# Three weight slots converted anew in the second pair, and output blocks that take PSUM banks 4 to 7 first

## The chip, the cores and the metric

The kernel runs on one core of a Trainium2 chip. The metric is the device time of one execution in microseconds (us). A smaller time is better.

## What is computed

Attention over local chunks (4 batches, 8 heads, 768 positions, head size 64, 8 memory positions), then two feed-forward layers over the 3072 rows that result:

```python
scores = scale * np.matmul(q_c, k_full.transpose(0, 1, 3, 2))   # chunks of 32, 16 left, 8 right, 8 memory
out[:, :, c_start:c_end] = np.matmul(softmax(scores), v_full)
...
h = x @ w_in                                  # [3072,512] @ [512,2048]
x = (h * np.tanh(softplus(h))) @ w_out        # [2048,512]
...
xn = x / rms * rms_g
g = xn @ w_gate                               # [512,1536]
return (silu(g) * (xn @ w_val)) @ w_out2      # [1536,512]
```

The weights arrive as 64-bit floats and are turned into 32-bit ones on the chip. Each matrix product is done with three matmuls, on a rounded high part and a low part of each operand (hi by hi, hi by lo, lo by hi).

## The kernel before

**Tiling.** The 3072 rows are 8 blocks of 384 and 4 pairs of blocks. A pair is multiplied with a pair of weight columns by a scheme of seven products in place of eight (`group`, from L572): products 1, 6, 5, 4, 2, 7, 3 in that order, on four PSUM banks X, Y, Z, V. VectorE, ScalarE and GpSimd take the results out. Seven products need seven weight blocks, each with a high and a low part: a weight slot of 1792 KB.

**The w_in slots.** The eight slots ("i", 0) to ("i", 7) share five places in SBUF (`W_SLOT`): 0 and 5 in place 0, 1 and 6 in place 4, 2 and 7 in place 3, slot 3 in place 2, slot 4 in place 1. A slot is first converted "plain" (`cv_all`): two 512 KB loads of raw 64-bit columns (tile raw, two buffers), and for each two ScalarE passes (L180, L183), three VectorE passes (L187, L188, L194) and a split into high and low parts (L140 ScalarE, L141 VectorE). That gives the four blocks themselves. `finish` (from L249) makes the other blocks out of them: it adds the halves back together (L254), forms four sums on GpSimd (L259, L260) and VectorE (L261, L262) and splits them. A job of the kind "pair" does all in one: two raw loads, conversion, sums and splits of seven blocks. Its block order is `W_AT`; that of a finished plain slot is `W_IN`.

**Stages.** A prologue starts the attention and the first products. *Stage 1* (about 60 to 156 us in the profile) multiplies pair 0 with plain slots, eight products by block (`unit`), with the attention of pair 1 between the products. *Stage 2* (156 to 246) is pair 1 over the slots 7 to 0 with the attention of pair 2 in between, *stage 3* (246 to 320) is pair 2 over 0 to 7 with the attention of pair 3, *stage 4* (320 to 390) is pair 3 over 7 to 1, with the conversion of w_out in between. Then come the w_out products of the 8 blocks (`out1`), which accumulate in four banks each (`banks1`), the gate and value products (`group2`) and the last product (`group3`).

**Order.** The function `between` that `slots` returns runs after each product (a step). It sends stores that are due, runs what `more` holds for that step, gives out attention pieces, and drives the conversion to a given count (`cv_upto`). The tile framework then orders each engine's instructions by a simulated time line, apart from those under `pin` or `in_start`; so a step is a place in the program and not a time.

**Places of slots.** In stage 1, `finish` of slots 0, 1, 2 stands right after their use, and `keep_w` stores each slot to DRAM (tensor wi) in two stores of 896 KB (L124). Slot 7 is finished at the end of stage 1, slots 6, 5, 4, 3 at steps 1, 8, 15, 22 of stage 2, where slots 7, 6, 5 are stored. `reload` (L119) loads the slots 2, 1, 0 in stage 2 after the first three groups, 5, 6, 7 in stage 3, and 2, 1, 0 again in stage 4.

**Queues.** All DMAs are issued by SyncE's queue (SP) in one order: raw loads (L136), loads of queries (L314), keys (L304), values (tile vw, eight loads of 56 KB a tile, L335), stores of products (g_scratch, L105), and stores and loads of slots.

**Banks.** Attention uses banks 4 to 7. The groups of pairs 1 to 3 use banks 0 to 3 (`group_banks(4)`); block m of w_out uses banks 0 to 3 if m is even and 4 to 7 if it is odd.

Of the kernel before, what the change touches and what calls it, by code (L numbers as in the profile page):

```python
# [24 lines left out]
W_AT = {1: 0, 2: 1, 4: 2, 3: 3, 5: 4, 6: 5, 7: 6}  # L25
W_IN = {1: 0, 2: 1, 3: 2, 4: 3, 5: 4, 6: 5, 7: 6}
# [3 lines left out]
def tile_kernel(  # L30
# [24 lines left out]
    N = 384  # L55
# [96 lines left out]
    def add_plain(key, arr, f0, f1, u):  # L152
        jobs.append(("plain", key, [(arr, "col", f0), (arr, "col", f1)], u, True, False))
# [348 lines left out]
    def att_list(j):  # L502

        out = []
        t0 = TPP * j
        for s in range(TPP + 4):
            for op, lag in (("e", 4), ("d", 3), ("c", 2), ("b", 1), ("a", 0)):
                t = t0 + s - lag
                if t0 <= t < t0 + TPP:
                    if op == "a" and t % SPB == 0:  # L510
                        out.append([(att_a0, t)])
                    out.append([(att_ops[op], t), (att_ops[op + "1"], t)])
        return out
# [45 lines left out]
    def product(at, w, t, bank_, first):  # L559
        ws = w[:, at].rearrange("p l (k f) -> p l k f", k=2)  # L560
        ps = bank_[:, 0:N]
        for kk in range(2):
            whi, wlo = ws[:, 0, kk, :], ws[:, 1, kk, :]
            xh, xl = t[:, 0, kk, :], t[:, 1, kk, :]
            more = dict(skip_group_check=not first)
            nc.tensor.matmul(ps, whi, xh, start=first and kk == 0, stop=False, **more)  # L566
            nc.tensor.matmul(ps, whi, xl, start=False, stop=False, **more)  # L567
            nc.tensor.matmul(ps, wlo, xh, start=False, stop=kk == 1, **more)  # L568
# [41 lines left out]
    def unit(b, i):  # L610
        need(("i", i))
        w = wtab["i", i]
        g = gp.tile([128, 2, N], F32, tag="g", name="g")
        for e in range(2):
            ps = bk[(2 * n_unit[0] + e) % 4]
            for half in range(2):
                product(2 * e + half, w, xtab[b, half], ps, half == 0)
                if half:
                    nc.scalar.copy(g[:, e, :], ps[:, 0:N])
                    if e:  # L620
                        store_later(
                            g_d[0, 2 * i:2 * i + 2, :, b, :].rearrange("f p n -> p f n"), g
                        )
                yield
        n_unit[0] += 1

    def run(parts, between):
        while parts:
            for part in list(parts):
                if next(part, "end") == "end":  # L630
                    parts.remove(part)
                else:
                    between()
# [3 lines left out]
    def group_banks(of):  # L637
        g = n_group[0]
        n_group[0] += 1
        return [bk[(4 * g + i) % of] for i in range(4)]  # L640

    def group1(j, i, between):
        run([group1_parts(j, i)], between)
# [1 line left out]
    def group1_parts(j, i):  # L645
        need(("i", i))
        g = [gp.tile([128, 2, N], F32, tag="g", name="g") for _ in range(2)]
        ts = {p: ttab_x[j, p] for p in ORDER}
        mul = lambda p, bank_, first: product(W_IN[p], wtab["i", i], ts[p], bank_, first)
        banks = group_banks(4)  # L650
        c11 = banks[0][:, 0:N]
        yield from group(mul, banks, N, g[0][:, 1, :], g[1][:, 0, :], g[1][:, 1, :])
        nc.scalar.copy(g[0][:, 0, :], c11)
        for e in range(2):
            store_later(g_d[j, 2 * i + e], g[e])
# [50 lines left out]
            return self.out.pop(0)  # L706

    def banks1(m):
        return [bk[(4 * m + c) % 8][:, 0:N] for c in range(KC)]

    def out1(m, i, t):
        for e in range(2):
# [96 lines left out]
    down = up[::-1]  # L809
    for i in (0, 1, 2, 3, 4, 5, 7, 6):  # L810
        add_plain(("i", i), w_in, 2 * i, 2 * i + 1, W_SLOT[i])
    for f, u in zip(range(0, F1, 3), (5, 6, 7, 1, 2, 3)):
        fs = range(f, min(f + 3, F1))
        add_rows([("o1", x) for x in fs], w_out, fs, u)
# [42 lines left out]
    def slots(pieces, conv, tail=(), more={}, cap=10 ** 6):  # L857


        state = dict(n=0, att=0, tail=0)  # L860
        plist, n_slots = pieces
        first_cv, to = conv
        base = cv_n[0]

        def between():
            state["n"] += 1
            n = state["n"]
            flush()
            if n in more:
                more[n]()  # L870
            span = n_slots - 7
            while state["att"] < len(plist) and state["att"] * span < n * len(plist):
                for fn, t in plist[state["att"]]:
                    fn(t)
                state["att"] += 1
            if n > first_cv:
                cv_upto(min(cap, base + (to - base) * (n - first_cv) // (n_slots - first_cv)))
            if n >= n_slots - 7 and tail:
                if state["tail"] == 0:
                    state["t"] = tail()  # L880
                    for fn in state["t"][0]:
                        fn()
                elif state["tail"] <= len(state["t"][1]):
                    state["t"][1][state["tail"] - 1]()
                state["tail"] += 1

        return between

    def tail_of(j):
        return lambda: t_pieces(j, xb.pop(2 * j), xb.pop(2 * j + 1), t_new, None, ttab_x)  # L890

    def keep_w(i, half):
        return lambda: w_store(("i", i), half)

    def reload(pos, seq):
        if pos < 3:
            w_load(("i", seq[5 + pos]), W_SLOT[seq[5 + pos]])
# [3 lines left out]
    def then(more, n, fn):  # L901
        more.setdefault(n, []).append(fn)

    def finish_at(more, i, n):
        part = finish(("i", i))
        for step in range(3):
            then(more, n + step, lambda: next(part))

    def calls(more):
        return {n: (lambda fns=fns: [fn() for fn in fns]) for n, fns in more.items()}  # L910
# [2 lines left out]
    units += [(b, i) for i in (2, 3, 4, 5, 7, 6) if i >= NHEAD for b in range(2)]  # L913
    at = {u: 4 * n + 4 for n, u in enumerate(units)}
    more = {}
    for i in range(3):
        finish_at(more, i, at[1, i] + 1)
        for half in range(2):
            then(more, at[1, i] + 4 + 3 * half, keep_w(i, half))
    finish_at(more, 7, at[1, 7] + 1)  # L920
    bt = slots((att_list(1), 4 * len(units)), (0, 73), tail_of(1), calls(more), CV_I)
    for b, i in units:
        run([unit(b, i)], bt)
    more = {}
    for i, ns in ((7, (3, 5)), (6, (9, 12)), (5, (16, 19))):
        for half, n in enumerate(ns):
            then(more, n, keep_w(i, half))
    for n, i in enumerate((6, 5, 4, 3)):
        finish_at(more, i, 7 * n + 1)
    bt = slots((att_list(2), 56), (0, 0), tail_of(2), calls(more))  # L930
    for pos, i in enumerate(down):
        group1(1, i, bt)
        reload(pos, down)
    bt = slots((att_list(3), 56), (0, 0), tail_of(3))
    for pos, i in enumerate(up):
        group1(2, i, bt)
        reload(pos, up)
    att_stack.close()
    w2p[0] = ctx.enter_context(
        tc.tile_pool(name="w2p", bufs=1, side="right", reuse_waits="tile")  # L940
# [173 lines left out]
```

## Time and profile before

| | us |
|---|---|
| median of three runs | 1208.36 (1205.7 to 1210.33) |
| the profiled execution | 1208.05 |
| its span in the profile | 1206.3 |
| TensorE busy in the span | 1164.7 (97%) |
| VectorE busy | 820.8 (68%) |
| ScalarE busy | 623.3 (52%) |
| GpSimd busy | 210.5 (17%) |

Busy times are of an engine's own instructions. What an idle stretch of TensorE (PE) waited for stands in brackets in a row of the time line: the time, and the instruction that ended the wait. PEclk is the granted clock of TensorE as a share of 2.4 GHz, which has two levels, 1.2 and 2.4 GHz; DMA is the mean busy share of the core's 16 DMA engines.

### The profile page before, as it was taken

How to read it: one execution, taken by the hardware profiler on the slowest of the kernel's cores; microseconds unless marked ns; L12 is line 12 of the kernel's file. 1: busy time of each engine (PE TensorE's matmuls, PEld its weight loads, DVE VectorE, ACT ScalarE, POOL GpSimd, SP SyncE). 2: the span in 40 equal slices, each digit the busy share in tenths (PEclk: the TensorE clock that was granted, in tenths of full speed). 3: DMA queues.
4: the chain of work that ended last, by engine and by line, in shares of the span. 5: the costliest groups of instructions: out<-in, count | busy, mean ns of one | idle time of the engine just before them, and what ended most of it. 6: DMA issues, size and time to landing. Idle time of an engine off the chain costs nothing.

```text
span 1206.3 us, 24873 instructions
## 1 busy us (share of the span) xinstructions
PE 1164.7 (97%) x9944; PEld 1128.4 (94%) x9944; DVE 820.8 (68%) x1331; ACT 623.3 (52%) x1055; POOL 210.5 (17%) x203
## 2 busy tenths in 40 slices
PE   5899889999999999999999999999999999999998
PEld 4788779888998999999999989999999999999998
DVE  3676695563676866668586876676667665987773
ACT  4565454343456874776866554443434433444442
POOL 2030131111134311111101222212122211100000
PEclk8799989999999999999999999999999999999999
DMA  9999889778387843858559788888397669755540
GB/s 184 207 260 268 223 253 295 206 215 248 104 345 268 294 146 121 324 176 300 192 179 410 289 335 341 321 331 332 109 356 276 267 223 337 190 161 141 141 132 36
DMA packets 216052, 287.50 MB, mean 238 GB/s; under 512 B 103552, under 2 KB 181376, under 8 KB 211712
## 3 DMA queue, kind: packets, MB, share of 16 engines
q1 hardware_dynamic: 215936, 285.91, 71.7%
q8 instruction: 78, 1.28, 0.4%
q14 instruction: 38, 0.31, 0.1%
HBM read 180.49 MB, written 105.38 MB: 237 GB/s over the span
## 4 chain that ended last, share of the span: by engine, by line
PE 81%; DMA 7%; DVE 6%; ACT 3%; issue 2%; SPq 1%; POOL 0%; DVEq 0%; ACTq 0%; POOLq 0%
PE bk L566 13%; PE bk L567 12%; PE bk L568 12%; PE bk L674 4%; PE bk L673 4%; PE bk L675 4%; PE bk L786 4%; PE bk L787 4%; PE bk L788 4%; DMA raw<-in_moe_w_in_dram 2%; PE bkp L566 2%; PE bkp L568 2%; PE bkp L567 2%; PE bkp L675 2%; PE bkp L674 2%; PE bkp L673 2%
## 5 line engine op out<-in xcount | busy, mean ns | idle before, releaser
L566 PE MATMUL bk<-T,w 128*128 128x384 f32 x992 | 340.3, 345 | 4.8 <-DMA T<-nt_scratch 1.8
L567 PE MATMUL bk<-T,w 128*128 128x384 f32 x992 | 335.1, 338 | 0.0
L568 PE MATMUL bk<-T,w 128*128 128x384 f32 x992 | 331.3, 337 | 0.1
L566 PEld LDWEIGHTS bk<-T,w 128*128 128x128 f32 x992 | 187.3, 189 | 10.6 <-DMA T<-nt_scratch 2.8
L567 PEld LDWEIGHTS bk<-T,w 128*128 128x128 f32 x992 | 187.7, 189 | 0.9
L568 PEld LDWEIGHTS bk<-T,w 128*128 128x128 f32 x992 | 186.9, 189 | 0.5 <-DVE w L141 0.4
L673 PE MATMUL bk<-T,w 128*128 128x384 f32 x384 | 130.6, 342 | 1.7 <-DVE s L593 1.7
L674 PE MATMUL bk<-T,w 128*128 128x384 f32 x384 | 129.9, 338 | 1.7 <-DVE T L141 1.7
L675 PE MATMUL bk<-T,w 128*128 128x384 f32 x384 | 129.4, 337 | 0.0
L786 PE MATMUL bk<-w,T 128*128 128x256 f32 x396 | 111.7, 282 | 0.0
L788 PE MATMUL bk<-w,T 128*128 128x256 f32 x396 | 111.4, 282 | 0.0
L787 PE MATMUL bk<-w,T 128*128 128x256 f32 x396 | 111.3, 281 | 0.0
L593 DVE TENSOR_TENSOR s<-bk,s 128x384 f32<-128x384 f32 (+1 forms) x84 | 45.0, 536 | 91.2 <-PE bk L568 81.7
L597 POOL TENSOR_TENSOR v<-s,z 128x384 f32<-128x384 f32 x48 | 53.2, 1109 | 193.5 <-DVE s L593 128.4
L141 DVE TENSOR_TENSOR T<-g,T 128x768 fp32r<-128x768 f32 x64 | 66.0, 1048 | 20.9 <-ACT T L140 20.8
L674 PEld LDWEIGHTS bk<-T,w 128*128 128x128 f32 x384 | 72.7, 189 | 3.1 <-DVE T L141 2.3
L787 PEld LDWEIGHTS bk<-w,T 128*128 128x128 f32 x396 | 75.5, 191 | 0.0
L673 PEld LDWEIGHTS bk<-T,w 128*128 128x128 f32 x384 | 72.6, 189 | 2.9 <-ACT ca L180 2.0
L786 PEld LDWEIGHTS bk<-w,T 128*128 128x128 f32 x396 | 75.2, 190 | 0.0
L141 DVE TENSOR_TENSOR T<-w,T 128x768 fp32r<-128x768 f32 x60 | 58.8, 991 | 23.9 <-ACT T L140 23.1
L788 PEld LDWEIGHTS bk<-w,T 128*128 128x128 f32 x396 | 75.1, 190 | 0.0
L140 ACT CAST T<-w 128x768 fp32r<-128x768 f32 x60 | 49.3, 833 | 47.5 <-PE bk L788 28.4
(158 smaller groups left out, 2358.1 us busy)
## 6 DMA issues: line engine op xcount, KB each, us to landing
T<-nt_scratch SPq DMA_DIRECT2D x49, 768.0 KB
g_scratch<-g SPq DMA_DIRECT2D x64, 384.0 KB
g<-g_scratch SPq DMA_DIRECT2D x64, 384.0 KB
h_scratch<-s SPq DMA_DIRECT2D x48, 384.0 KB
w<-h_scratch SPq DMA_DIRECT2D x24, 768.0 KB
w<-wi SPq DMA_DIRECT2D x9, 1792.0 KB
nt_scratch<-T SPq DMA_DIRECT2D x21, 768.0 KB
raw<-in_moe_w_out_dram SPq DMA_DIRECT2D x28, 512.0 KB
```

The lines of the kernel that those rows point to most:

```text
L140: keep(nc.scalar.copy(hi, src))
L141: keep((eng or nc.vector).tensor_tensor(lo, src, hi.bitcast(F32), op=ALU.subtract))
L566: nc.tensor.matmul(ps, whi, xh, start=first and kk == 0, stop=False, **more)
L567: nc.tensor.matmul(ps, whi, xl, start=False, stop=False, **more)
L568: nc.tensor.matmul(ps, wlo, xh, start=False, stop=kk == 1, **more)
L597: nc.gpsimd.tensor_tensor(c22, u3, z5, op=ALU.add)
L673: nc.tensor.matmul(ps, ahi, bhi, start=start, stop=False)
L674: nc.tensor.matmul(ps, ahi, blo, start=False, stop=False)
L675: nc.tensor.matmul(ps, alo, bhi, start=False, stop=stop)
L786: nc.tensor.matmul(ps, t[:, 0, f], w[:, 0], start=first and f == 0, stop=False, **more)
L787: nc.tensor.matmul(ps, t[:, 0, f], w[:, 1], start=False, stop=False, **more)
L788: nc.tensor.matmul(ps, t[:, 1, f], w[:, 0], start=False, stop=f == HG - 1, **more)
```

## The change

Slots 0, 1 and 2 are no longer finished and stored in stage 1. They are dropped after their plain use and converted again from the raw columns by three "pair" jobs, which stand in the conversion's order between the plain jobs and w_out. Those 33 steps of conversion are spread over steps 12 to 45 of stage 2; the reloads of stage 2 go. The finishes of slots 6, 5, 4, 3 move to steps 1, 4, 7, 10. Slots 0, 1, 2 are stored in stage 3, at steps 1 to 17, for the reloads of stage 4. From stage 2 on these three slots are read in the order `W_AT`. The three entries that do nothing (`lambda: None`) add nothing.

Blocks of w_out with an even m take banks 4 to 7, those with an odd m banks 0 to 3, and the groups with eight banks begin with 4 to 7 in place of 0 to 3. `group_banks(4)` gives the same banks as before.

```diff
-        return [bk[(4 * g + i) % of] for i in range(4)]
+        return [bk[(4 * g + of - 4 + i) % of] for i in range(4)]
...
-        mul = lambda p, bank_, first: product(W_IN[p], wtab["i", i], ts[p], bank_, first)
+        at = W_AT if i < 3 else W_IN
+        mul = lambda p, bank_, first: product(at[p], wtab["i", i], ts[p], bank_, first)
...
     def banks1(m):
-        return [bk[(4 * m + c) % 8][:, 0:N] for c in range(KC)]
+        return [bk[(4 * m + 4 + c) % 8][:, 0:N] for c in range(KC)]
...
+    for i in (2, 1, 0):
+        add_pair(("i", i), w_in, 2 * i, w_in, 2 * i + 1, W_SLOT[i], True, False)
...
-    for i in range(3):
-        finish_at(more, i, at[1, i] + 1)
-        for half in range(2):
-            then(more, at[1, i] + 4 + 3 * half, keep_w(i, half))
     finish_at(more, 7, at[1, 7] + 1)
...
+    for i in range(3):
+        del wtab["i", i]
...
     for n, i in enumerate((6, 5, 4, 3)):
-        finish_at(more, i, 7 * n + 1)
-    bt = slots((att_list(2), 56), (0, 0), tail_of(2), calls(more))
-    for pos, i in enumerate(down):
+        finish_at(more, i, 3 * n + 1)
+    for n, i in ((8, 2), (15, 1), (22, 0)):
+        then(more, n, lambda: None)
+    bt = slots((att_list(2), 56), (12, CV_I + 33 + 11), tail_of(2), calls(more), CV_I + 33)
+    for i in down:
         group1(1, i, bt)
-        reload(pos, down)
-    bt = slots((att_list(3), 56), (0, 0), tail_of(3))
+    more = {}
+    for i, ns in ((0, (1, 3)), (1, (8, 10)), (2, (15, 17))):
+        for half, n in enumerate(ns):
+            then(more, n, keep_w(i, half))
+    bt = slots((att_list(3), 56), (0, 0), tail_of(3), calls(more))
...
+    CV_I += 33
```

## Rows read from the trace of the kernel before

**Rows 1.** The page: the span.
```profile
span 1206.3 us, 24873 instructions
```
**Rows 2.** Stages: window, its length, busy us (instructions) of each engine, clock, DMA.
```profile
60.00:110.00 50.00, 49.14 (x713) 45.74 (x713) 37.40 (x76) 33.88 (x64) 9.15 (x10) 1.00 0.91 268
110.00:156.00 46.00, 36.77 (x534) 33.01 (x540) 29.77 (x52) 20.94 (x40) 8.41 (x8) 0.95 0.88 225
156.00:246.00 90.00, 88.04 (x1231) 80.14 (x1212) 59.54 (x112) 41.58 (x77) 15.73 (x18) 0.97 0.84 255
246.00:320.00 74.00, 72.57 (x1103) 66.03 (x1104) 35.77 (x74) 27.45 (x50) 7.57 (x7) 1.00 0.68 199
390.00:1206.00 816.00, 806.40 (x5080) 801.15 (x5080) 573.69 (x871) 428.04 (x705) 138.56 (x127) 1.00 0.67 239
```
**Rows 3.** Time line of TensorE, 110 to 157 us: start, length, instruction, [wait before].
```profile
119.64 0.66 PE L490 MATMUL bk<-ident,x 128*128 128x128 f32 x4 [1.67 <-ACT qT L405]
...
137.52 0.79 PE L490 MATMUL bk<-ident,x 128*128 128x128 f32 x4 [1.57 <-DVE x L480]
...
155.70 0.89 PE L415 MATMUL bkp<-kw,qT 64*32 64x64 f32 x38 [3.81 <-DVE kw L360]
```
**Rows 4.** Waits of ScalarE, 60 to 156 us: total, times, longest.
```profile
ACT ca L180 <- DMA raw<-in_moe_w_in_dram: 15.5, 6, 5.7
```
**Rows 5.** The chain that ended last, 100 to 140 us: start, length, what.
```profile
111.47 6.41 DMA raw<-in_moe_w_in_dram
...
134.31 3.95 DMA raw<-in_moe_w_in_dram
```
**Rows 6.** Time line of SP's queue, stages 1 and 2: start, time to issue, what.
```profile
102.06 0.69 SPq L124 DMA_DIRECT2D wi<-w  x1
102.84 7.43 SPq L335 DMA_DIRECT2D vw<-in_v_dram  x8
110.33 1.04 SPq L124 DMA_DIRECT2D wi<-w  x1
...
128.31 5.89 SPq L335 DMA_DIRECT2D vw<-in_v_dram  x8
...
149.42 1.70 SPq L335 DMA_DIRECT2D vw<-in_v_dram  x4
...
208.99 10.60 SPq L335 DMA_DIRECT2D vw<-in_v_dram  x8
```
**Rows 7.** DMA view of 80 to 112 us.
```profile
DMA packets 10299, 9.30 MB, mean 291 GB/s; under 512 B 7321, under 2 KB 9639, under 8 KB 10294
```
**Rows 8.** VectorE's groups, 60 to 110 us: count, busy us, mean ns, idle before.
```profile
L188 DVE SCALAR_TENSOR_TENSOR ca<-raw,ca 128x512 int32<-128x512 int32 x6 | 4.1, 686 | 0.1
L194 DVE CUSTOM_DVE_ANT_0 ca<-ca,lr 128x1024 uint16<-128x1024 uint16 x6 | 4.1, 684 | 0.2
L141 DVE TENSOR_TENSOR w<-sm,w 128x768 fp32r<-128x768 f32 (+1 forms) x6 | 3.9, 680 | 0.0
...
L187 DVE TENSOR_SCALAR ca<-ca 128x512 int32<-128x512 int32 x6 | 2.5, 409 | 2.8 <-ACT ca L180 2.8
```
**Rows 9.** Stretches of 10 us around both changes of stage, columns as in rows 2.
```profile
150.00:160.00 10.00, 5.95 (x83) 4.60 (x82) 9.20 (x12) 6.49 (x12) 4.30 (x3) 0.75 0.94 276
160.00:170.00 10.00, 10.00 (x112) 9.23 (x112) 10.00 (x21) 5.30 (x11) 1.44 (x2) 0.91 0.48 144
...
390.00:400.00 10.00, 9.48 (x46) 9.51 (x47) 8.57 (x12) 8.20 (x14) 5.41 (x4) 0.83 0.90 309
```
**Rows 10.** Time line of VectorE at the change to stage 2.
```profile
151.28 1.92 DVE L141 TENSOR_TENSOR w<-sm,w 128x768 fp32r<-128x768 f32 x2
```
**Rows 11.** Time line of TensorE late in stage 2.
```profile
229.55 1.38 PE L464 MATMUL bkp<-vw,pT 64*32 64x65 f32 x12 [1.24 <-DMA vw<-in_v_dram]
```
**Rows 12.** Time lines of TensorE and VectorE at the first w_out block.
```profile
390.52 0.66 PE L673 MATMUL bk<-T,w 128*128 128x384 f32 x1 [1.70 <-DVE s L593]
...
388.95 0.96 DVE L141 TENSOR_TENSOR T<-g,T 128x768 fp32r<-128x768 f32 x1 [2.16 <-ACT T L140]
```

## The prediction

> **What bounds the kernel now.** I read the stages first [rows 1, 2]. TensorE is busy for 1164.7 us of 1206.3 by the table, and its work isn't changed by more than bank numbers. So all that the change can win is idle time and time at the lower clock, in the places that it touches. From 390 us on, 806.40 of 816 us are busy; before 60 us nothing is touched. Between lie these losses: 0.9 us in 60 to 110, 9.2 us in 110 to 156, 2.0 in stage 2, 1.4 in stage 3 (each is the window's length less PE busy).
>
> Then I looked at what ended those waits. In 110 to 156 there are four waits before 140 us (1.67 us the first, 1.57 the last), each for a different ScalarE or VectorE result, and one of 3.81 us at 155.70 [rows 3]. The four come to 5.0 us. Behind all four is one thing: ScalarE stands at L180 and waits for raw columns, 15.5 us in six times, 5.7 the longest [rows 4]. An engine that works in order holds back everything queued behind such a wait, here the evictions and the attention's copies that TensorE needs. The chain of waits says the same: it runs through the raw loads, 6.41 us from issue to landing at 111.47, 3.95 us at 134.31 [rows 5]. And SP's queue tells why they are issued late: right ahead of the one at 111.47 stand two slot stores (0.69 and 1.04 us) and, between them, eight value loads that took 7.43 us [rows 6].
>
> The wait at 155.70 is of another kind. It is VectorE's queue at the change of stage: key copies for the attention stand behind the sums of the next pair and behind a finish, of which two splits alone take 1.92 us [rows 10]. After it the clock is at the lower level: 0.75 and 0.91 in the two stretches [rows 9] make 2 x (0.25 + 0.09) x 10 = 6.8 us at 1.2 GHz, about 6 of them with TensorE at work, so 3.0 us more are lost.
>
> **The change part by part.** Sums are made against the profiled execution's 1208.05 us, 0.3 us under the median of 1208.36.
>
> *Stage 1, stores and finishes removed.* Six stores of 896 KB go, 5.4 MB. All DMA of 80 to 112 us is 9.30 MB at 291 GB/s [rows 7], so they are some 18 of those 32 us (5.4 / 9.3 of them). On SP's queue the raw load at 111.47 comes at least 0.69 + 1.04 = 1.7 us earlier. The value loads between are not of fixed length either: 0.93 us each there, 0.43 each at 149.42 with fewer transfers about, 1.33 each at 208.99 [rows 6]. At 0.43 the eight take 3.4 us in place of 7.4, 4.0 us more. So the raw load comes 1.7 to 5.7 us earlier, and each later one hangs on the one before. The four waits (5.0 us) shrink by 1.7 to 5.0; I take 4.0, nearer to the upper end since most of the bytes about are gone. With them goes time at the lower clock: 0.95 over 46 us [rows 2] is 4.6 us at that level, most of it right after the fourth wait and partly idle; I take 0.7 us, of 0 to 0.9. The finishes taken out free VectorE of 3.9 us of splits [rows 8] and the sums before them in 60 to 110, where TensorE lost only 0.9 us: nothing gained. Together **-4.7**, from -1.7 to -5.9.
>
> *Change to stage 2.* Slot 7's finish stays where it is. If the conversions end earlier, its passes come before the last attention tile and not in the middle of the sums; if the finishes of 5 and 4, now at steps 4 and 7, are drawn forward, one more pair of splits (1.92 us) stands ahead of the key copies. Bounds: +1.9 to -6.8 (the 3.8 us of idle time and the 3.0 us of clock). Nothing shows which, so I take a small part, **-1.3**. The four finishes packed into 12 steps fall where VectorE is busy 10.00 of 10 us already with TensorE busy 10.00 too [rows 9]: a full VectorE alone didn't stall it. **+0.3**, from 0 to 1.9.
>
> *Stage 2, three conversions added.* Each raw half costs VectorE 0.41 + 0.69 + 0.68 = 1.78 us [rows 8]; two halves, two small sums and four splits at about 0.68 or a little less make about 7 us a slot, 21 us in all. VectorE's 59.54 of 90 us [rows 2] become 80, or 89%. ScalarE, at 41.58 of 90, has more room still, and GpSimd's two sums a slot only move from stage 1 to here. By the 10.00 of rows 9 the added work itself is hidden. What can stall is what stalls in stage 1: a raw load that comes late. The first two are issued in stage 1, where w_out's stood. Each later one is issued when its buffer is read, and is wanted ten steps later, at some 90/56 = 1.6 us a step 16 us later; in stage 1 it was eight steps, 13 us. Value loads of 7 us ahead of it and a landing of 6.4 us make 13 to 14. So it was short there and just suffices here. **+1.0**, from 0 to 5.0, what the same cause costs in stage 1.
>
> *Stage 2, reloads removed.* Three loads, 5.4 MB, become six raw loads, 3.1 MB. The value loads that take 10.60 us at 208.99 should fall back to about 7, and the wait for values at 229.55, 1.24 us [rows 11], with them. SP no longer stands at L119 until a group has released its place. **-1.2**, from 0 to -1.2.
>
> *Stage 3, stores added.* The 5.4 MB come at steps 1 to 17, beside loads of 5.4 MB; DMA is at 0.68 there and TensorE loses 1.4 us now [rows 2]. It becomes what stage 2 is today: **+0.5**, from 0 to 1.2 (the one value wait of rows 11). The reloads of stage 4 find the data there long before.
>
> *Banks.* At the first w_out block TensorE waits 1.70 us until 390.52, for the reading of a bank of the last group [rows 12]. With banks 4 to 7, unused since stage 3, it needs only the operand T, whose low half is ready at 388.95 + 0.96 = 389.91. So 0.6 us are won if it must wait for that, 1.7 if the order lets it start with the high half, and the clock's 0.83 behind it [rows 9], 3.4 us at the lower level and 1.7 lost, may stay away too. I take **-0.7**, from -0.6 to -3.4. Later blocks alternate as before: nothing.
>
> Sum: -4.7 - 1.3 + 0.3 + 1.0 - 1.2 + 0.5 - 0.7 = -6.1, 1208.05 - 6.1 = **1202.0**.
>
> **The rivals.**
> 1. *SP's issue time is the limit, whatever the bytes.* Then the value loads of stage 1 stay at 7 us, the raw loads come 1.7 us earlier and no more, nothing is won at the change of stage or at 229.55: -1.7 + 0.3 + 1.0 + 0.5 - 0.7 = -0.6, **1207.5**. For it: eight such loads still take 5.89 us at 128.31, after the last store [rows 6]. Against it: 0.43, 0.93 and 1.33 us for one and the same load. The Trainium skill, "Perfetto Trace Analysis", section "What DMA-bound means", has this as its second case: an issuer's track that is solid DMA slices is bound by the making of descriptors and not by data movement. By that rule the time is the one above; the spread of rows 6 speaks against it here. Chance 0.22.
> 2. *The wait moves to stage 2* (slower). Six raw loads come in where slot stores of 7, 6, 5, product stores and value loads already go. If a raw load lands later than 16 us after its buffer is free, ScalarE stands at L180 with evictions of all four banks behind it, as in stage 1, where four raw loads cost 5.0 us, 1.25 each. Six cost 7.5 us, and the clock falls as it did at 155 us, 3.0 more: 10.5 in place of 1.0. With the value wait kept too (+1.2), -6.1 + 9.5 + 1.2 = +4.6, **1212.7**. For it: value loads of 10.60 us in this stage today. Against it: fewer bytes and longer steps. Chance 0.13.
> 3. *The change of stage closes up.* If slot 7's finish is over before the last attention tile, the sums start at once, and both the idle time and the clock loss go nearly whole: -6.0 in place of -1.3, **1197.3**. Against it: other finishes are drawn forward into the gap. Chance 0.15.
> 4. *It doesn't do what it says.* The framework orders engines by its own time line; the moved steps may land where they were, and gains and losses cancel: **1208**. Chance 0.05.
>
> **How the numbers follow.** The forecast has 0.45, its own range 1199 to 1205 (terms half a step to either bound). Below 1196.5 I leave 0.08 (rival 3 with the clock at the first w_out block), above 1211 0.12 (most of rival 2). A measurement can tell 0.5% from no change, 6.0 us: faster means below 1202.3. Of the forecast a little over half lies there, with rival 3 that makes 0.42; slower (above 1214.4) is the upper half of rival 2 and what I overlook, 0.09; the rest, 0.49, is within.
>
> **What would show it.** Right: no or short waits of L180 before 140 us, no wait over 1 us in 110 to 140; the first w_out matmul waits for T and not for a group's result; no wait for values near 229 us; VectorE near 90% in stage 2 with TensorE's idle time under 2 us. Wrong: L180 waiting for w_in in 160 to 230 us (rival 2), value loads of 0.9 us each still in stage 1 (rival 1). The forecast hangs most on stage 1 and on the change of stage, where VectorE's order is made by the framework and can't be read from here.

## The result, and the profile after

The changed kernel takes 1191.17 us (median of six, 1188.33 to 1195.78) beside 1210.36 for the kernel before in the same session (1205.7 to 1215.05): a ratio of 0.9872, 95% interval 0.9843 to 0.9901. That is faster by 1.3%, and it lies below the range of the prediction, 1196.5 to 1211. The sign was right, and the size was low by 11 us. The profiled execution took 1190.82 us, 17.2 less than that of before.

Where the time came from is read best from points of the program that both kernels pass: the starts of the groups of a pair, of the w_out blocks and of the later products. My count of the matmul records in the two profiles, in us:

| stretch | before | after | change | forecast |
|---|---|---|---|---|
| before the first w_in product | 44.50 | 45.22 | +0.7 | 0 |
| from there to the first group of pair 1 (stage 1 and the wait at its end) | 112.01 | 102.30 | -9.7 | -6.0 |
| stage 2 | 89.35 | 83.70 | -5.65 | +0.1 |
| stage 3 | 83.15 | 83.83 | +0.7 | +0.5 |
| stage 4, to the first w_out matmul | 61.51 | 59.96 | -1.55 | -0.7 with the next |
| first w_out block | 34.95 | 33.91 | -1.0 | |
| the other w_out blocks | 240.67 | 241.50 | +0.8 | 0 |
| gate and value products and the last product | 535.74 | 533.87 | -1.9 | 0 |

The forecast of -6.0 is the prediction's -4.7 and -1.3; part of the latter is clock at the start of stage 2. The last two kinds of product stand in one row because they overlap: 24 matmuls of the gate and value products run after the first matmul of the last product in before, and 6 in after. At the end of stage 1, 38 score matmuls of the attention (the last row of [rows 3], 0.89 us) run ahead of the border in before and behind it in after. By this count stage 3 of before ends at 329.0 us, and not at 320.

How far such lengths repeat is read from the kernels below whose edits leave a stage alone: there every engine has the same instructions in the same order. Stage 1 of after takes 102.30 to 104.44 us in six profiles (after, e2, e8, e12, e13, e15) and 107.13 in a seventh (e7); that of before takes 111.38 to 115.93 in three (before, e1, e6). Stage 2 of after takes 83.48 to 84.59 in four (after, e2, e9, e12), that of before 87.28 to 89.35 in the same three. So both stages are shorter beyond chance. The differences of the means are 9.3 and 4.6 us, and a difference of a us or two between two profiles means nothing.

The stages of the kernel after, by windows (columns as in [rows 2]):

```profile
60.00:110.00 50.00, 49.14 (x715) 45.68 (x714) 29.76 (x61) 32.72 (x61) 4.40 (x4) 1.00 0.88 232
110.00:148.00 38.00, 34.84 (x515) 32.52 (x514) 29.40 (x50) 19.84 (x36) 8.29 (x8) 1.00 0.82 195
148.00:232.00 84.00, 83.78 (x1197) 77.23 (x1196) 76.80 (x146) 51.84 (x98) 20.53 (x23) 0.98 0.83 249
232.00:316.00 84.00, 83.36 (x1196) 76.22 (x1195) 45.84 (x89) 35.11 (x63) 9.41 (x9) 1.00 0.78 246
376.00:1189.00 813.00, 804.10 (x5077) 799.34 (x5077) 575.13 (x871) 427.70 (x705) 139.98 (x127) 1.00 0.68 240
```

TensorE's idle time in 60 us to the end of stage 1 fell from 10.1 to 4.0 us, in stage 2 from 2.0 to 0.2. VectorE is at 76.80 of 84 us in stage 2, 91%, and TensorE loses nothing by it. In stage 1 DMA moves less: 232 and 195 GB/s in place of 268 and 225 [rows 2].

The time line of TensorE at the change to stage 2 and at the first w_out block:

```profile
147.52 0.44 PE L566 MATMUL bk<-T,w 128*128 128x384 f32 x1 [2.92 <-ACT g L619]
...
376.00 0.44 PE L675 MATMUL bk<-T,w 128*128 128x384 f32 x1 [0.20 <-DVE T L141]
```

Between 63 and 148 us this is the only wait over 0.25 us. The four before 140 us are gone, and the 3.81 us at the change [rows 3] became 2.92. At the first w_out block the 1.70 us for the reading of a bank [rows 12] became 0.20 for T. The clock, in stretches of 10 us around the change:

```profile
140.00:150.00 10.00, 6.84 (x70) 5.62 (x69) 10.00 (x17) 6.36 (x13) 2.82 (x3) 0.91 0.93 236
150.00:160.00 10.00, 10.00 (x88) 8.42 (x92) 9.86 (x17) 7.40 (x14) 1.43 (x2) 0.92 0.68 225
```

0.91 and 0.92 make 3.4 us at 1.2 GHz, where [rows 9] had 6.8. But for the last microseconds of the kernel it is the only lower stretch after 60 us; before had 13.6 us of them, 3.4 each after the waits around 135 us and at the first w_out block besides.

ScalarE's longest waits, 60 to 146 us, by what they waited for (total, times, longest):

```profile
ACT g L619 <- PE bk L568: 11.4, 12, 2.7
ACT pT L454 <- PE bk L447: 4.6, 5, 1.4
ACT w L140 <- DVE ca L194: 4.3, 4, 2.7
```

It waits for its producers now. The wait of L180 for raw columns, 15.5 us in [rows 4], is not in the list at all. SP's queue, the value loads of stage 1 and one of stage 2:

```profile
85.48 4.56 SPq L335 DMA_DIRECT2D vw<-in_v_dram  x8
95.96 3.70 SPq L335 DMA_DIRECT2D vw<-in_v_dram  x8
106.92 5.83 SPq L335 DMA_DIRECT2D vw<-in_v_dram  x8
118.03 4.46 SPq L335 DMA_DIRECT2D vw<-in_v_dram  x8
...
206.75 4.70 SPq L335 DMA_DIRECT2D vw<-in_v_dram  x8
```

Eight took 7.43 us at 102.84 and 10.60 at 208.99 [rows 6]. The four such rows of stage 1 average 4.6 us now and 6.6 before, the four of stage 2 5.8 and 9.2. Such a row also holds the queue's waits between the loads. Of the 7.43 us, 4.6 are issuing and 1.9 a wait until a slot store had landed; of the 10.60, 5.6 are issuing and 4.1 a wait until a reload had landed. SP's waits in stage 2 of before name the reloads (156 to 246 us):

```profile
SPq L335 <- DMA w<-wi: 6.8, 2, 4.1
```

In the trace, SP's DMAs take eight semaphores in turn, and these loads waited for the DMA that had the same one before. So a large transfer that lands late holds up the small ones behind it. Most single value loads take SP 0.32 to 0.5 us to issue, in before and in after.

Stage 2 holds a surprise: most of what it lost wasn't idle time. The stage between its two first groups in before, then in after (windows, columns as in [rows 2]):

```profile
156.51:245.86 89.35, 87.39 (x1195) 79.66 (x1192) 58.89 (x112) 40.93 (x75) 15.67 (x17) 0.97 0.84 255
```

```profile
147.52:231.22 83.70, 83.48 (x1195) 76.93 (x1195) 76.50 (x145) 51.54 (x97) 20.53 (x23) 0.98 0.83 248
```

With equally many records, TensorE is *busy* for 3.9 us less, and idle for 1.7 us less. The costliest groups of its instructions show where (lines view; busy us, mean ns, idle before), before and then after:

```profile
L566 PE MATMUL bk<-T,w 128*128 128x384 f32 x112 | 41.1, 368 | 0.3 <-ACT g L653 0.3
L567 PE MATMUL bk<-T,w 128*128 128x384 f32 x112 | 39.0, 348 | 0.0
L568 PE MATMUL bk<-T,w 128*128 128x384 f32 x112 | 38.4, 343 | 0.0
L464 PE MATMUL bkp<-vw,pT 64*32 64x65 f32 x384 | 6.8, 225 | 1.4 <-DMA vw<-in_v_dram 1.4
```

```profile
L566 PE MATMUL bk<-T,w 128*128 128x384 f32 x113 | 40.6, 359 | 3.1 <-ACT g L619 2.9 <-ACT g L654 0.2
L567 PE MATMUL bk<-T,w 128*128 128x384 f32 x112 | 38.4, 343 | 0.0
L568 PE MATMUL bk<-T,w 128*128 128x384 f32 x112 | 38.0, 340 | 0.0
...
L464 PE MATMUL bkp<-vw,pT 64*32 64x65 f32 x384 | 5.2, 225 | 0.0
```

The value products (L464) took 6.8 us and take 5.2: besides the 1.4 us marked as a wait for values, 1.6 us lay between matmuls that follow each other and were counted as busy (the 12 of [rows 11] alone take 1.38 us, where a whole tile of 64 takes 0.86 elsewhere). The matmuls of the groups went from 118.5 to 117.0. Of that the clock explains some 0.9: within the stage, before had 5.3 us at 1.2 GHz and after 3.4, and half of the difference is lost. So of stage 2's 5.65 us some 3.0 are late values, 0.9 the clock and the rest, about 1.7, is scattered.

### The profile page after: what moved, and what is told of

Read it like the earlier page. It is cut to its first block, busy times and chain, and to the rows that moved or that the text cites. A ratio compares the mean times of both kernels' runs of the same rounds, so it can differ in the third digit from the quotient of the medians.

```text
span 1189.0 us, 24942 instructions
## 1 busy us (share of the span) xinstructions
PE 1155.8 (97%) x9944; PEld 1121.8 (94%) x9944; DVE 831.8 (70%) x1349; ACT 632.4 (53%) x1073; POOL 212.0 (18%) x203
## 4 chain that ended last, share of the span: by engine, by line
PE 73%; DMA 9%; DVE 9%; ACT 6%; issue 3%; SPq 0%; DVEq 0%; ACTq 0%
PE bk L566 14%; PE bk L567 13%; PE bk L568 13%; PE bk L789 4%; PE bk L787 4%; PE bk L788 4%; DMA nt_scratch<-T 2%; DVE T L141 2%; DMA T<-nt_scratch 2%; PE bkp L566 2%; PE bkp L568 2%; PE bkp L567 2%; PE bkp L415 2%; DMA g<-g_scratch 2%; ACT T L140 2%
## 5 line engine op out<-in xcount | busy, mean ns | idle before, releaser
L566 PEld LDWEIGHTS bk<-T,w 128*128 128x128 f32 x992 | 186.7, 189 | 10.1 <-ACT g L619 3.2
L568 PEld LDWEIGHTS bk<-T,w 128*128 128x128 f32 x992 | 186.3, 188 | 0.2
L789 PE MATMUL bk<-w,T 128*128 128x256 f32 x396 | 111.6, 283 | 0.4 <-DVE T L141 0.4
```

The lines of the kernel that those rows point to most:

```text
L789: nc.tensor.matmul(ps, t[:, 1, f], w[:, 0], start=False, stop=f == HG - 1, **more)
```

## The experiments

The theory after the result: DMA bytes are what both stages lost time to. The stores of stage 1 and the reloads of stage 2 make the raw columns and the values late. (The median of before differs by session, 1207 to 1210 us, so the ratios are what is compared.) Its rivals were the finishes (VectorE's and GpSimd's passes), the number of issues on SP's queue whatever their bytes, and SP's queue standing at a reload until a group gives its place free. Where an experiment adds a store, it goes to a tensor that nothing reads; where it adds a load, nothing uses the data.

Since the framework orders each engine's instructions itself, the traces tell what an edit really changed. In the stage that is edited, e9 and e13 keep the order of after on every engine but SP; e3, e7, e10 and e15 don't. Stage lengths are of one profile each.

**e1_banks: before with the banks changed alone.**

```diff
-        return [bk[(4 * g + i) % of] for i in range(4)]
+        return [bk[(4 * g + of - 4 + i) % of] for i in range(4)]
...
-        return [bk[(4 * m + c) % 8][:, 0:N] for c in range(KC)]
+        return [bk[(4 * m + 4 + c) % 8][:, 0:N] for c in range(KC)]
```

> The kernel before with the change of banks alone. If the first w_out block waited for banks of the last group, its first matmul now starts right behind the last group (gap under 0.6 us in place of 1.9) and the clock stays high behind it: 2 to 3 us less than before, all of it between the last group and the second w_out block. If the wait was for the operand T, the gap stays near 1.2 us or more, the clock falls as before, and the time is that of before within 1 us.

1201.52 us, ratio 0.9935 (0.9910 to 0.9961). Stage 4 to the first w_out matmul is 59.97 us in place of 61.51, the first block 33.90 in place of 34.95, the gate and value products with the last product 534.44 in place of 535.74: 3.9 us, of which I had only looked for the first two. The interval allows 4.7 to 10.9 us. Up to the end of stage 3, where the program is that of before, this profile is 2.1 us shorter too, which is chance.

**e2_nobanks: after with the old banks** (the diff of e1 reversed).

> The changed kernel with the old banks. If the parts add up, it loses the 2 to 3 us that the banks alone gain: some 13 us under before, and TensorE's wait of 1.5 to 2 us at the first w_out block is back. If the two parts need each other, it stands near before or near the changed kernel.

1193.63 us, ratio 0.9882 (0.9838 to 0.9926): the runs don't tell it from after. TensorE's time line at the first w_out block has the wait back:

```profile
376.52 0.42 PE L674 MATMUL bk<-T,w 128*128 128x384 f32 x1 [1.70 <-DVE s L593]
```

The gate and value products with the last product take 535.42 us, as with the old banks in before and e6 (535.74 and 535.95). Of the thirteen kernels with the new banks twelve have 533.0 to 534.4, and e4 has 536.5. The clock didn't fall behind the wait this time (first block 33.40 us). So in the profiles the banks are worth some 2 to 4 us: the wait, some 2 us in the products behind w_out and, in some executions, the clock. By e1's runs it is at least 4.7.

**e3_stores: after with the six stores of stage 1 put back**, without the finishes.

```diff
+    def spare_w(i, half):
+        return lambda: pin(nc.sync.dma_start(
+            out=spare_d[i][:, half * SLOT // 2:(half + 1) * SLOT // 2],
+            in_=wslot["i", i][:, 0:SLOT // 2].bitcast(F32)))
...
+    for i in range(3):
+        for half in range(2):
+            then(more, at[1, i] + 4 + 3 * half, spare_w(i, half))
```

> The changed kernel with six stores of 896 KB put back into stage 1 at their old steps, to a tensor that nothing reads. Theory 1 (the stores delay the raw loads, through the DMA engines and SP's queue): ScalarE waits for raw columns again, some 10 us or more in 60 to 146 us, TensorE's waits of some 4 to 6 us come back before the change of stage, and the time rises by 5 to 8 us over the changed kernel. Theory 2 (the finishes in VectorE's and GpSimd's order were the cause): no such waits, and the time rises by less than 1.5 us.

1199.23 us, ratio 0.9919 (0.9897 to 0.9942). Stage 1 is 111.55 us, 9.25 more than in after, stage 2 stays at 83.57. Some 1 us of the 9.25 is 48 score matmuls that now run ahead of the border. TensorE is idle for 9.1 us of the stage (4.4 in after). ScalarE's wait for raw columns is back (waits, 60 to 150 us), and so are value loads of 7 us:

```profile
ACT ca L182 <- DMA raw<-in_moe_w_in_dram: 18.6, 6, 5.5
```

```profile
87.41 7.71 SPq L337 DMA_DIRECT2D vw<-in_v_dram  x8
...
102.31 7.25 SPq L337 DMA_DIRECT2D vw<-in_v_dram  x8
```

**e4_finishes: after with the finishes of slots 0 to 2 back in stage 1, and e5_both: with finishes and stores.**

```diff
+    for i in range(3):
+        finish_at(more, i, at[1, i] + 1)
```

> The changed kernel with the finishes of slots 0, 1, 2 put back into stage 1 at their old steps; their results are not used. Theory 1 (stores): no wait of ScalarE for raw columns beyond 2 us, time within 1.5 us of the changed kernel. Theory 2 (finishes): TensorE's waits before the change of stage come back, 4 to 8 us over the changed kernel.

> The changed kernel with both the six stores and the finishes of slots 0 to 2 put back into stage 1. Stores alone made stage 1 9.3 us longer (111.6 us from the first product to the first group of pair 1, changed kernel 102.3, before 112.0), finishes alone 3.0. If both act through the same thing, the late raw loads, stage 1 takes 112 us again and no more, 8 to 9 us over the changed kernel. If they are separate costs, it takes 114 us or more.

e4: 1196.69 us, ratio 0.9894 (0.9865 to 0.9923), single runs from 1190.9 to 1200.6. Stage 1 is 105.27 us, stage 2 85.88. e5: 1199.28 us, ratio 0.9935 (0.9910 to 0.9959); stage 1 is 112.16. So stage 1 takes 102.3 with neither, 105.3 with the finishes, 111.6 with the stores, 112.2 with both (before: 112.0). The stores are the larger cause, and the order of instructions in e5's stage 1 is that of before. What the finishes cost alone isn't shown: 105.3 lies among the lengths that stage 1 of after takes by chance, the runs of e4 aren't told apart from after's, and on top of the stores they add 0.6. In e4 the wait at the end of the stage is for VectorE's key copies again (TensorE's time line), and L180 waits for raw columns once, 2.9 us:

```profile
148.78 0.71 PE L415 MATMUL bkp<-kw,qT 64*32 64x64 f32 x46 [2.23 <-DVE kw L360]
```

**e6_fin3n: before with the finishes of slots 6, 5, 4, 3 at steps 1, 4, 7, 10.**

```diff
-        finish_at(more, i, 7 * n + 1)
+        finish_at(more, i, 3 * n + 1)
```

> The kernel before with the finishes of slots 6, 5, 4, 3 at steps 1, 4, 7, 10 of stage 2 and nothing else. If the earlier finishes made stage 2 shorter (89.4 us before, 83.7 in the changed kernel), it takes 85 to 87 us here. If they only fill VectorE at the change of stage, as I took them in the sum, stage 2 stays at 88 to 91 us and the time within 2 us of before.

1208.15 us, ratio 1.0014 (0.9996 to 1.0031): no gain. Stage 2 is 87.28 us, stage 1 115.93. But this edit moved nothing: all engines and SP's queue have the same instructions in the same order in both traces. The framework puts a finish where its own time line wants it, whatever the step. So this is a second set of runs of before, and no test of earlier finishes. The traces settle the question in another way: the last split of the finishes ends 28.6 us into stage 2 in before and 28.5 in after, so they don't come earlier in after. The reverse, after with the finishes at their old steps, was not tried: they and the pair conversions take the same buffers.

**e7_reloads: after with three loads of 1792 KB at the old places of stage 2's reloads.**

```diff
-    for i in down:
+    for pos, i in enumerate(down):
         group1(1, i, bt)
+        if pos < 3:
+            s = w_slot(W_SLOT[down[5 + pos]])
+            nc.sync.dma_start(out=s.bitcast(I32), in_=w_in[128 * pos:128 * pos + 128, 0:SLOT // 2].bitcast(I32))
```

> The changed kernel with three loads of 1792 KB put back into stage 2 after the first three groups, into the places of slots 2, 1, 0; the data are not used and the conversions overwrite them. If the reloads (bytes, and SP standing until a group has released its place) made stage 2 long, it takes 87 to 90 us again, with a wait of TensorE for values or for results that stand behind a late raw load, 3 to 6 us over the changed kernel. If not, it stays within 1 us of 83.7.

1200.63 us, ratio 0.9960 (0.9940 to 0.9981), 9.5 above after. Stage 2 is 90.52 us, 6.8 more, with a wait of 1.23 us for values and ScalarE's waits for raw columns (waits, 156 to 250 us):

```profile
ACT ca L180 <- DMA raw<-in_moe_w_in_dram: 6.2, 3, 2.8
```

Stage 3 is longer too, 88.89 us; that part is not explained. Stage 1, where the program is that of after, is longer by chance (107.13 us, with a wait of 2.87 us for keys that after doesn't have): the profiled run is one of the slower of the nine (1204.54). In this kernel two things are mixed: the bytes, and SP's queue and the conversions standing at the places that are loaded. e13 and e15 below were meant to take them apart.

**e8_fin5: after with those finishes at steps 5, 8, 11, 14** (`3 * n + 5`).

> The changed kernel with the finishes of slots 6, 5, 4, 3 four steps later, at steps 5, 8, 11, 14 of stage 2. At the change to stage 2 TensorE still waits 2.9 us, for bank copies on ScalarE behind a split that waits for VectorE's sums; slot 6's finish runs on VectorE and GpSimd in that stretch. If it is in the way, the wait falls to some 1 us and the clock stays high: 2 to 4 us less than the changed kernel. If the sums' own length sets it, nothing changes; if the later finishes hold up the conversions, 1 to 3 us more.

1194.26 us, ratio 0.9908 (0.9871 to 0.9944), not told apart from after. The wait at the change of stage stays at 2.85 us, for the same copy of ScalarE. This doesn't try slot 6's finish, though: from 141 to 156 us VectorE, ScalarE and GpSimd have the same instructions in the same order as in after, and only later finishes moved. What holds the wait up can be read from after itself. The copy stands in ScalarE's queue behind the split of a sum, and that split waited for VectorE (time line of ScalarE in after):

```profile
146.25 0.83 ACT L140 CAST T<-t 128x768 fp32r<-128x768 f32 x1 [2.61 <-DVE t L543]
146.99 0.47 ACT L619 COPY g<-bk 128x384 f32<-128x384 f32 x1
```

**e9_tiny: e3 with stores of 64 bytes a partition.**

```diff
-            out=spare_d[i][:, half * SLOT // 2:(half + 1) * SLOT // 2],
-            in_=wslot["i", i][:, 0:SLOT // 2].bitcast(F32)))
+            out=spare_d[i][:, half * SLOT // 2:half * SLOT // 2 + 16],
+            in_=wslot["i", i][:, 0:16].bitcast(F32)))
```

> As the run with the six stores put back into stage 1, but each store moves 64 bytes a partition (8 KB) and not 896 KB: SP issues as many DMAs at the same places, with hardly any bytes. Stage 1 takes 102.3 us in the changed kernel and 111.6 with the full stores. If the bytes on the DMA engines made the raw loads late, it takes 102 to 104 us and ScalarE waits under 3 us for raw columns. If SP's issuing (one queue, in order) did, it takes 107 us or more.

1191.17 us, ratio 0.9858 (0.9836 to 0.9880). Stage 1 is 103.50 us. L182 waits for raw columns once (60 to 142 us), and the two value loads that took 7.71 and 7.25 us in e3 take 4.46 and 5.61:

```profile
ACT ca L182 <- DMA raw<-in_moe_w_in_dram: 2.0, 1, 2.0
```

```profile
85.57 4.46 SPq L337 DMA_DIRECT2D vw<-in_v_dram  x8
...
95.61 5.61 SPq L337 DMA_DIRECT2D vw<-in_v_dram  x8
```

The four rows of the stage average 5.5 us, 7.0 in e3 and 4.6 in after. Without their bytes the six issues cost nothing that can be told from chance: 103.50 us is among the lengths of after's own stage 1, and the ratio is within the interval of e12 below, which is after in the same session. With the bytes the stage is 9.25 us longer. A part of these can come from the other order of instructions in e3; a kernel with the bytes and the order of after was not run.

**e10_actq: e3 with the stores issued by ScalarE** (`nc.scalar.dma_start` in place of `nc.sync.dma_start`).

> As the run with the six full stores put back into stage 1, but issued from ScalarE's queue and not from SP's. If the bytes are the cause, stage 1 takes 109 to 113 us as with SP's stores. If SP's order is, it takes 102 to 105 us, apart from what ScalarE loses by issuing.

1198.67 us, ratio 0.9919 (0.9894 to 0.9943). The ratio is that of e3. Stage 1 is 107.50 us, 5.2 above after and 4.0 below e3, in a profile of the fastest of the four runs (1195.28). L182 waits for raw columns in four pieces, 7.0 us. So the bytes cost time even where the raw loads don't stand behind the stores on one queue. It is not clean: ScalarE itself stood for 5.29 us once, ahead of 93.10, until a value load had landed, with one of the stores issued right before its next copy.

**e11_tail: after with the sums of the next pair begun one step later.**

```diff
-            if n >= n_slots - 7 and tail:
+            if n >= n_slots - 6 and tail:
```

> The changed kernel with the sums of the next pair (the tail of a stage) begun one step later. If the 2.9 us wait at the change to stage 2 comes from the splits of these sums standing ahead of bank copies in ScalarE's queue, the wait falls to 1.5 us or less and the time by 1 to 4 us. If the sums' length sets it, the wait grows by up to 1 us at each of the changes of stage, and the time by 1 to 3 us.

1189.85 us, ratio 0.9844 (0.9823 to 0.9866): the same as after's 0.9846 in that session (e12). Stage 1 shrinks to 97.64 us and stage 2 grows to 88.70: together 186.3, as in after's second run (186.0). The wait only moved behind the border that I count by (TensorE's time line):

```profile
147.13 0.44 PE L566 MATMUL bk<-T,w 128*128 128x384 f32 x1 [2.97 <-ACT T L140]
```

**e12_again: after once more**, without an edit.

> The changed kernel once more, for how far two profiles and two sets of runs of one kernel differ. If the differences of stages read so far are real, stage 1 takes 102 to 103.5 us, stage 2 83 to 85, and the ratio to the kernel before is 0.984 to 0.990. If they are chance, stage 1 differs by 3 us or more.

1189.61 us, ratio 0.9846 (0.9829 to 0.9863). Stage 1 is 102.49 us and stage 2 83.49, as expected of real differences. The other kernels with the same program in these stages differ by more.

**e13_tinyload: e7 with loads of 64 bytes a partition.** SP's queue still has to wait until the place is free, and the conversion into it for the load.

```diff
-            nc.sync.dma_start(out=s.bitcast(I32), in_=w_in[128 * pos:128 * pos + 128, 0:SLOT // 2].bitcast(I32))
+            nc.sync.dma_start(out=s[:, 0:16].bitcast(I32), in_=w_in[128 * pos:128 * pos + 128, 0:8].bitcast(I32))
```

> After, with the three loads of stage 2 put back at their old steps and into their old places, but of 64 bytes a partition (data that nothing uses). SP's queue again has to stand until a group has given its place free, and the conversions into these places have to wait for the load; hardly a byte moves. Stage 2 took 83.5 to 83.7 us in after, 90.5 with full loads (e7) and 88.6 to 89.4 in before. Theory A (the bytes of the reloads are what stage 2 loses to): stage 2 stays at 83.5 to 85 us, no wait for values over 0.5 us, total 1190 to 1192. Theory B (SP standing at the place's release, with value and raw loads behind it, is the loss): stage 2 at 87 us or more, a wait for values or for raw columns back, total 1194 to 1198.

1189.92 us, ratio 0.9866 (0.9839 to 0.9893). Stage 2 is 84.31 us, among the lengths of after's own. Nothing of e7's 6.8 us can be told from chance, and the order of instructions is that of after. But theory B was hardly tried: SP stood at a place's release for 0.8 us, once, where it had stood for 5.9 in before (SP's waits in stage 2, before and then e13):

```profile
SPq L119 <- PE bk L568: 5.9, 1, 5.9
```

```profile
SPq L938 <- PE bk L568: 0.8, 1, 0.8
```

**e15_stage2stores: after with six more stores of 896 KB in stage 2**: the bytes of the reloads, with no place to wait for (`spare_w` as in e3, from slot 4).

```diff
+    for n, i in ((11, 0), (18, 1), (25, 2)):
+        for half in range(2):
+            then(more, n + 2 * half, spare_w(i, half))
```

> After, with six stores of 896 KB more in stage 2 (slot 4 to a tensor that nothing reads, at steps 11 to 27): the bytes of the reloads, 5.4 MB, on SP's queue, but no place that has to come free and no conversion that has to wait for them. Theory A (bytes): stage 2 rises by 4 to 7 us to 87.5 to 90.5, as stage 1 rose by 9 with the same six stores, value loads of more than 0.9 us each and a wait for values or raw columns; total 1195 to 1199. Theory B (SP standing): stage 2 rises by under 1.5 us, total 1190 to 1193.

1201.58 us, ratio 0.9963 (0.9946 to 0.9980). Stage 2 is 93.17 us, 9.5 more than in after. Three value loads of eight take 7.91, 7.85 and 8.06 us on SP's queue. The time lines of ScalarE and TensorE show how the late transfers reach the matmuls:

```profile
213.01 0.67 ACT L182 ACTIVATE ca<-raw 128x512 f32<-128x512 f32 x1 [3.78 <-DMA raw<-in_moe_w_in_dram]
216.21 0.48 ACT L656 COPY g<-bk 128x384 f32<-128x384 f32 x1 [1.97 <-DMA g_scratch<-g]
```

```profile
216.75 0.68 PE L568 MATMUL bk<-T,w 128*128 128x384 f32 x1 [2.18 <-ACT g L656]
```

First ScalarE stands for a raw half, then for a buffer of results whose store hasn't landed, and behind that copy TensorE stands for its bank. e15 shows that the bytes, with no place to wait for, can cost stage 2 more than the 5.65 us in question; e13 shows that three loads without bytes cost nothing. Two things stay open. In e15 the engines' order is another one than in after, with 68 matmuls more between the two borders, and what that costs by itself was not measured. And SP's 5.9 us at a place's release in before may have had a part.

## Why the prediction was right in sign and wrong in size

**Stage 1: the mechanism right, a size off.** The four waits went, as forecast, with the raw loads coming earlier when fewer bytes move: e3 and e10 bring the waits for raw columns back with the bytes, and e9 without them hardly does. Measured -9.7 where -6.0 was forecast (-4.7 and -1.3). Between the borders of the stage TensorE's idle time fell by 6.1 us (10.5 to 4.4) and its busy time by 3.6 (101.6 to 97.9). About 1 of the 3.6 is the 38 score matmuls that moved behind the border and no gain. Most of the rest is the clock, which was capped at 0.9 us: the stage held 6.2 us at 1.2 GHz in before, 3.4 around 135 us and the rest at its end, and 0.7 in after. "The finishes taken out ... nothing gained" stands, since e4 shows no cost of them beyond chance.

Two readings were off. The 0.93 and 1.33 us of [rows 6] aren't what one value load takes to issue, since these rows hold SP's waits for slot transfers too; that more of the bytes gone would shorten them was right all the same. And eight of the 52 steps of stage 1 take some 15 us of its 96, not 13.

**The change to stage 2: near, in part by luck.** The prediction said that nothing shows which way this goes and took a small part. A wait of 3.81 us became one of 2.92 for another instruction, and half of the clock loss stayed. The third rival, that the gap closes up, came true only in the clock's half. What holds the rest is the split that waits for VectorE's sums (the lines under e8); with the sums a step later the wait was 2.97 us (e11).

**Stage 2: the step that failed.** It was forecast at +0.1 and came out at -5.65 (-4.6 by the means of the profiles). Two terms were wrong. The three conversions cost nothing in place of +1.0: L180 has no wait for raw columns there, and VectorE at 91% leaves TensorE 0.2 us of idle time. The removed reloads were priced at -1.2, the one wait for values that the trace marked, with that as the bound. e7 and e15 put 6.8 and 9.5 us on the same bytes, with the order that came with them. The step behind both is in the first paragraph of the prediction: it took the 2.0 us of idle time as about all that stage 2 could give back. In fact 3.9 of its 5.65 us had been counted as busy: gaps between the matmuls of the value products (1.6), the clock behind the change of stage (0.9), and small ones that I could not sort out.

**Stage 3: right.** +0.7 for +0.5.

**Banks: too low.** "Later blocks alternate as before: nothing" was wrong. The gate and value products with the last product are some 2 us shorter with the new banks. In before TensorE waits three times where the gate and value products of the second pair begin, 1.24, 0.82 and 0.59 us at 717.50 to 723.64, and in after once for 0.17; but such waits differ between profiles (1.43 us in e1), and how they hang on the banks I didn't find. The first w_out block gave 1.55 us and the clock 1.0, inside the bounds of 0.6 to 3.4.

**The rivals.** The first, SP's issue time as the limit whatever the bytes, falls by the value loads of stage 1, which went from 6.6 us for eight to 4.6 on average with as many loads, and by e9 (six issues without bytes, no cost that shows). The Trainium skill, "Perfetto Trace Analysis", section "What DMA-bound means", reads an issuer's solid track as a limit of descriptor making and would have put SP's rows of stages 1 and 2 down to that. Here a part of them was no issuing at all but waits for slot transfers to land, and the rest too got shorter with fewer bytes. The second, a wait that moves to stage 2, did not come: value loads shrank as in stage 1. The fourth falls with the result.

**What stays open.** Time and bytes aren't in a fixed ratio. From the mean rates of the windows stage 2 moved 22.8 MB before and 20.8 after (255 GB/s by 89.35 us, 248 by 83.70): 2.0 MB less for 5.65 us, of which 0.9 are clock. e15 adds 5.4 MB for 9.5 us. Which transfers collide seems to decide, and I have no rule for it. How much of a stage's loss is the transfers alone and how much the order that the framework makes of them, what SP's standing at a place cost in before, and how the banks' 2 to 4 us divide over executions are open too.

## What to carry to other kernels

Price a transfer that is removed by what its bytes do to everything else in flight in that stage, and not by the one wait that names it; to see that price, put a store of the same size and then one of 64 bytes a partition at the same place. Compare the order of each engine's instructions in the traces before such a pair is read: where a framework makes the order, an edit can move nothing (e6), or more than was meant (e3, e15). A row of several loads on a queue's time line is not only issuing; look for the waits in it. A TensorE that is 97% busy can still have time to give back: compare its busy time for the same matmuls in a loaded stage and in a quiet one before its idle time is called the most that can be won. Converting again cost nothing here, because VectorE could go from 66% to 91% of the stage without a wait for it.

## What the runs showed of the hardware

- Most 56 KB loads take SP's queue 0.32 to 0.5 us to issue, in before and in after. What made rows of eight of them 7.43 and 10.60 us long in before were single issues of up to 1.40 and 2.03 us and waits until a slot store (1.9 us) or a reload (4.1 us) had landed.
- Six stores with 8 KB each left stage 1 at 103.50 us and the ratio at 0.9858 (e9), six with 896 KB each at the same places made it 111.55 us and 0.9919 (e3; a part can be the other order of instructions). Issued from ScalarE's queue the full stores cost as much time (0.9919, e10).
- The same program's stage 1 took 102.30 to 107.13 us in seven profiles, its stage 2 83.48 to 84.59 in four.
- For 1195 matmul records each, TensorE counted as busy for 87.39 us in stage 2 of before and 83.48 in that of after.
